# Second layers of a mixture of experts on one core: one product of 160 columns in place of two of 80, and a VectorE addition of the halves

## Chip, cores and metric

One Trainium2 chip, one core of it. The metric is the device time of one execution in microseconds (us). A profile is one such execution, recorded by the hardware; its times count from the start of the span.

## What is computed

Causal attention over 8 batches, 12 heads, 448 positions and 64 dimensions, in f32, and behind it a mixture of 8 experts over the 3584 resulting rows of 768:

```python
logits = x @ w_gate                       # 3584 x 8
expert_idx = np.argmax(logits, axis=1)    # one expert a row, softmax weight gate_w
for e in range(8):
    tok_idx = rows of expert e, at most the 80 with the largest gate_w
    h = np.maximum(x[tok_idx] @ w1[e], 0.0)             # 768 -> 1024, first layer
    out[tok_idx] = gate_w[tok_idx, None] * (h @ w2[e])  # 1024 -> 768, second layer
```

All other rows of the output are zero. The weights are f32, 768 x 1024 and 1024 x 768 an expert.

## The kernel before

**Two stages.** Up to about 325 us the core computes attention, the routing and the choice of rows; then it runs the experts' layers. The change lies in this second stage alone. There each layer is computed with weights as the stationary operand: TensorE loads a 128 x 128 block of a weight chunk (128 rows of the weight matrix, 1024 columns in a first layer, 768 in a second) and multiplies it with the 80 chosen tokens as 80 columns. A first layer has 6 chunks of 8 blocks, a second layer 8 chunks of 6 blocks.

**Split weights.** So as to multiply in f16 at f32 accuracy, weights and activations are split into a high and a low half. For a chunk ScalarE makes `wh` = f16(32 w) (L1203, "high"), VectorE makes `wl` = 32 w - wh (L1209, "low"). Of the tokens, `xh`/`xl` (first layer, L1443 and L1449) and `hh`/`hl` (second layer, L1460 and L1466) are the halves. Each block then takes three products of 80 columns, L1504 to L1506: `wh` with the high half, `wh` with the low half, `wl` with the high half, summed in PSUM. Each product is two TensorE instructions, a weight load and a matmul. The last chunk of seven layers (`WHOLE`) isn't split and goes as one f32 product a block (L1501).

**Around a layer.** Tokens are gathered by POOL (L1417) and turned by TensorE (`xtp`). A second layer's sum lies in one bank of PSUM, tile `op` (128 x 480, two buffers); ScalarE copies it to SBUF (`yt`, L1528), TensorE turns it back (`ytp`), ScalarE weights it (`yo`), POOL scatters it. The last expert (`last_layer`) does its last three chunks by halves of the output, and VectorE copies the second half (L1523).

**Buffers.** Raw weights come in pieces of three first-layer or four second-layer chunks into 11 buffers (L348, 74 loads in this stage, issued by SP); a load into a region waits until the high and low of the chunk that was there are made. There are 12 buffers for `wh` and 11 for `wl`; each is free when its chunk's products are done.

**Order.** `plan_experts` writes out the order of TensorE's, ScalarE's, VectorE's and SP's instructions by a simulation with the costs of the table `COST` (ns) and a due place in TensorE's order for each operation. TensorE's order of layers is first layer of expert 0, first of 1, second of 0, first of 2, second of 1 and so on: the layers of two experts alternate. On the chip each engine then runs its instructions in this order and waits on semaphores; so an operation that stands too early in an engine's order holds up all behind it.

Of the kernel before, what the change touches and what calls it, by code (L numbers as in the profile page):

```python
# [7 lines left out]
F32 = mybir.dt.float32  # L8
F32R = mybir.dt.float32r
F16 = mybir.dt.float16  # L10
BF16 = mybir.dt.bfloat16
I32 = mybir.dt.int32
AF = mybir.ActivationFunctionType
ALU = mybir.AluOpType
# [3 lines left out]
P = 128  # L18
# [30 lines left out]
ROW_ENGINES = "ppappppa"  # L49

COST = {"hi1": 950, "hi2": 735, "lo1": 1135, "lo2": 870, "xw": 210, "xh": 460, "xl": 575, "hw": 120, "hh": 330, "hl": 400,
        "yt": 470, "yo": 490, "xtp": 420, "ytp": 660, "warm": 600, "split": 108, "whole": 224, "ld": 460, "far": 2100, "seen": 100, "slack": 900}
BEGIN = {"ACT": 400, "SP": 1500, "DVE": 5900, "PE": 9400}
GATHERED, GATHERS = [9400, 12500, 14500], 6000

# [1 line left out]
def plan_experts(E, layers, blocks, order, whole, early, pieces, loaded, buffers, his, los, ready_h, ready_l):  # L57

    pe = [("xtp", 0), ("warm", 0)]
    for e, w in layers:  # L60
        for x, c in enumerate(order[e, w]):
            n = len(order[e, w])
# [7 lines left out]
    at = {op: i for i, op in enumerate(pe)}  # L70
    splits = [op[1:] for op in pe if op[0] == "p" and not whole(*op[1:]) and op[1:] not in early]
    ops, by = {}, []

    def add(op, engine, cost, needs, when):
        ops[op] = engine, COST[cost] if isinstance(cost, str) else cost, [d for d in needs if d], when
    used = {}
    for op in pe:
        if op[0] == "p":
            _, e, w, c = op
            o = whole(e, w, c)  # L80
            needs = [(("xw" if w == 1 else "hw") if o else ("xl" if w == 1 else "hl"), e), ("ld" if o else "lo", e, w, c)]
            if order[e, w][0] == c and e >= 2:
                needs.append(("hl" if w == 1 else "yt", e - 2))
            add(op, "PE", blocks[w] * COST["whole" if o else "split"], needs, at[op])
        elif op[0] == "warm":
            add(op, "PE", "warm", [], at[op])
        else:
            add(op, "PE", op[0], [("got", op[1]) if op[0] == "xtp" else ("yt", op[1])] + by, at[op])
            by = [("xl", op[1])] if op[0] == "xtp" else [("yo", op[1])]
    for e in range(E):  # L90
        for w, hi, lo, raw in ((1, "xh", "xl", "xw"), (2, "hh", "hl", "hw")):
            after = ("xtp", e) if w == 1 else ("p", e, 1, order[e, 1][-1])
            cs = {o: [at["p", e, w, c] for c in order[e, w] if whole(e, w, c) == o] for o in (False, True)}
            if cs[True]:
                add((raw, e), "ACT", raw, [after], min(cs[True]) - 0.5)
            if cs[False]:
                n = 2 if w == 2 else 1
                add((hi, e), "ACT", n * COST[hi], [after], min(cs[False]) - 0.7)
                add((lo, e), "DVE", n * COST[lo], [(hi, e)], min(cs[False]) - 0.5)
        if e < E - 1:  # L100
            add(("yt", e), "ACT", "yt", [("p", e, 2, order[e, 2][-1])], at["ytp", e] - 0.5)
            add(("yo", e), "ACT", 2 * COST["yo"], [("ytp", e)], at["ytp", e] + 4)
    done = {("lo", *y): 0 for y in early}
    for i, (e, w, c) in enumerate(splits):
# [17 lines left out]
    busy, times, ends, out, gathers = dict(BEGIN), set(BEGIN.values()), {}, [], len(GATHERED)  # L122
# [21 lines left out]
    while times:  # L144
        t = min(times)
# [4 lines left out]
        while empty and coming < len(pieces):  # L150
            held[coming] = empty.pop(0)
            e, w, cs = pieces[coming]
            for j, c in enumerate(cs):
                op = ("ld", e, w, c)
# [22 lines left out]
def attention_then_moe(  # L177
# [12 lines left out]
    nc = tc.nc  # L190
    B, _, NP, S = qT.shape
    N, D = out.shape
    E = wg.shape[2]
# [4 lines left out]
    NC1 = D // P  # L198
# [49 lines left out]
    SL = max(2, min(P, CAP))  # L248
# [9 lines left out]
    OFF, at = {}, 0  # L258
# [48 lines left out]
    def whole(e, which, c):  # L307

        return c == (NC1, NC2)[which - 1] - 1 and ((e, which) in WHOLE if AHEAD else e < E - which % 2 - 1)
# [3 lines left out]
    ORDER, sooner, PIECES = {}, [], []  # L313
    for x, (e, which) in enumerate(LAYERS):
        cs = sorted(range((NC1, NC2)[which - 1]), key=lambda c: (not whole(e, which, c), c))
        k = (K1, K2)[which - 1]
        if x in AHEAD:
            sooner.append((e, which, cs[:k]))
            PIECES.append((e, which, cs[k:]))
            cs = [c for both in zip(cs[:k], cs[k:]) for c in both]  # L320
        else:
            PIECES += [(e, which, cs[i:i + k]) for i in range(0, len(cs), k)]
        ORDER[e, which] = cs
    SOONER = [(e, which, c) for e, which, cs in sooner for c in cs]
    PIECES = sooner + PIECES
# [825 lines left out]
    n = len(pairs)  # L1151
# [33 lines left out]
    SW, SX = 32.0, 8.0  # L1185
# [5 lines left out]
    def source(y):  # L1191
        if y not in raw_of:
            i, j = place_of[y]
            raw_of[y] = chunk_of(wload[i], len(PIECES[i][2]), j)
        return raw_of[y]
# [48 lines left out]
    for i, pr in enumerate(pairs):  # L1244
# [13 lines left out]
        h = i // PH  # L1258
# [13 lines left out]
        _, first, afters = scores  # L1272
# [98 lines left out]
    for i, x in enumerate(ROW_ENGINES):  # L1371
        g, t = divmod(i, NT)
# [29 lines left out]
    ffn = ctx.enter_context(tc.tile_pool(name="ffn", bufs=2, side="right", reuse_waits="tile"))  # L1402
    ps_m = ctx.enter_context(tc.tile_pool(name="ps_m", bufs=2, space=PSUM, reuse_waits="tile"))
    ps = ctx.enter_context(tc.tile_pool(name="ps", bufs=2, space=PSUM, reuse_waits="tile"))
    NF = F // P
# [3 lines left out]
    PER = NC1 if NC1 * SL <= 512 else NC1 // 2  # L1409
# [12 lines left out]
    class Unit:  # L1422
# [32 lines left out]
            nc.scalar.activation(self.w2, self.hp[-1][:, HALF - n:], AF.Relu, scale=SW)  # L1455

        def hh(self):
            self.h2 = ffn.tile([P, NF, SL], F16, name="hh", tag="hh")
            for i, t in enumerate(self.hp):
                nc.scalar.activation(self.h2[:, i * HALF:(i + 1) * HALF], t, AF.Relu)  # L1460

        def hl(self):
            self.l2 = ffn.tile([P, NF, SL], F16, name="hl", tag="hl")
            for i, t in enumerate(self.hp):
                part = slice(i * HALF, (i + 1) * HALF)
                nc.vector.scalar_tensor_tensor(out=self.l2[:, part], in0=t, scalar=0.0, in1=self.h2[:, part], op0=ALU.max,  # L1466
                                               op1=ALU.subtract)

        def banks(self, which):
            if which == 1:  # L1470
                self.per = HALF
                self.hp = [ps.tile([P, HALF, SL], F32, name="hp", tag="h", bufs=4) for _ in range(2)]
                return self.hp
            final = self.e == E - 1
            self.per = NC1 // 2 if final else PER
            if final:
                self.op = [ps.tile([P, PER, SL], F32, name="op", tag="o")[:, 0:self.per],
                           ps.tile([P, HALF, SL], F32, name="hp", tag="h", bufs=4)[:, 0:self.per]]
            else:
                self.op = [ps.tile([P, self.per, SL], F32, name="op", tag="o", padded_shape=[P, PER, SL])  # L1480
                           for _ in range(NC1 // self.per)]
            return self.op

        def product(self, which, c, part=None):

            n = (NC1, NC2)[which - 1]
            blocks = (NF, NC1)[which - 1]
            x = ORDER[self.e, which].index(c)
            if x == 0 and not part:
                self.out = self.banks(which)  # L1490
            y = self.e, which, c
            if not whole(*y):
                h, l = (self.h1, self.l1) if which == 1 else (self.h2, self.l2)
                wh, wl = hi_of[y], lo_of[y]
            for i in part or range(blocks):
                o = self.out[i // self.per][:, i % self.per, :]
                ws = slice(i * P, (i + 1) * P)
                begin, end = x == 0 and i % self.per == 0, x == n - 1
                if whole(*y):
                    w = self.w1 if which == 1 else self.w2  # L1500
                    nc.tensor.matmul(o, source(y)[:, ws], w[:, w.shape[1] + c - n, :], start=begin, stop=end,  # L1501
                                     skip_group_check=True)
                    continue
                nc.tensor.matmul(o, wh[:, ws], h[:, c, :], start=begin, stop=False, skip_group_check=True)  # L1504
                nc.tensor.matmul(o, wh[:, ws], l[:, c, :], start=False, stop=False, skip_group_check=True)  # L1505
                nc.tensor.matmul(o, wl[:, ws], h[:, c, :], start=False, stop=end, skip_group_check=True)  # L1506

        def last_layer(self, c):
# [15 lines left out]

        def yt(self):
            self.y = ffn.tile([P, NC1, SL], F32, name="yt", tag="yt")
            for i, t in enumerate(self.op):
                nc.scalar.activation(self.y[:, i * self.per:(i + 1) * self.per], t, AF.Copy, scale=1.0 / (SW * SW * SX))  # L1528

        def ytp(self):  # L1530
            self.tp = []
# [22 lines left out]
    for s in range(NSL):  # L1554
# [7 lines left out]
        bufs = wload[0:BUFS]  # L1562
# [6 lines left out]
        for (kind, e, *y), info in turns:  # L1569
# [5 lines left out]
            elif kind == "ld":  # L1575
                b, i, j = info
# [7 lines left out]
            elif kind == "warm":  # L1584
                if PER == NC1:
                    warm = ps_m.tile([P, PER * SL], F32, name="wp", tag="misc")
# [53 lines left out]
```

## Time and profile before

| | us |
|---|---|
| median of 3 runs | 446.72 (446.46 to 448.32) |
| profiled execution | 446.64 |
| its span | 444.6 |
| TensorE busy in the span | 419.5 (94%) |
| ScalarE busy | 388.3 (87%) |
| VectorE busy | 379.3 (85%) |

The profiled execution is the one whose rows are shown; 2.04 us of it lie outside the span. Its granted TensorE clock is 0.994 of full speed, so the clock plays no part in what follows. The shares are means over two unlike stages; the stage of the experts is read by itself.

### The profile page before, as it was taken

Reading aid. Unit: us, or ns where it says so; the run is one execution under the profiler, and the core shown is the slowest. Engines: PE = TensorE matmul, PEld = TensorE weight load, DVE = VectorE, ACT = ScalarE, POOL = GpSimd, SP = SyncE. Lnnn points to the kernel's source line nnn. Section 1 sums busy time; section 2 is a strip of 40 time slices with the busy share of each in tenths; the row PEclk is TensorE's granted clock in tenths of the full one; section 3 lists DMA queues with packets and bytes.
Section 4 is the critical chain, followed back from the end, with each engine's and each line's share of the span. In section 5 each row is a group of like instructions: output and inputs, shape, how many; then the busy total and the mean of one; then the engine's idle time right before and its main releaser. Section 6 shows DMA issues by size and latency. Waiting matters only on the chain.

```text
span 444.6 us, 15877 instructions
## 1 busy us (share of the span) xinstructions
PE 419.5 (94%) x5847; PEld 325.2 (73%) x5847; DVE 379.3 (85%) x1302; ACT 388.3 (87%) x1062; POOL 286.9 (65%) x439
## 2 busy tenths in 40 slices
PE   7899999999999999999999999999789999888894
PEld 3666777677777777767777777766469999887893
DVE  6777788979889898988998989888879999989791
ACT  5899999999989999998999998978868979878891
POOL 7967998998898898899889885412462242210021
PEclk9899999999999999999999999999999999999999
DMA  7485668859786974976664387199359999999701
GB/s 224 147 272 184 195 227 285 291 201 295 241 282 199 290 242 152 297 253 212 214 215 144 124 243 272 66 349 312 126 171 349 403 403 411 393 414 413 306 27 46
DMA packets 49869, 109.95 MB, mean 247 GB/s; under 512 B 5970, under 2 KB 27474, under 8 KB 49152
## 3 DMA queue, kind: packets, MB, share of 16 engines
q1 hardware_dynamic: 48592, 105.20, 68.4%
q0 software_dynamic: 1056, 3.51, 2.4%
q8 instruction: 46, 0.75, 0.7%
q14 instruction: 31, 0.25, 0.2%
q10 hardware_dynamic: 144, 0.23, 0.2%
HBM read 85.35 MB, written 23.99 MB: 246 GB/s over the span
## 4 chain that ended last, share of the span: by engine, by line
PE 83%; ACT 5%; DVE 4%; issue 3%; POOL 2%; DMA 1%; POOLq 0%; DVEq 0%; ACTq 0%
PE xp L662 18%; PE tp L638 17%; PE sp L580 12%; PE rt L773 4%; ACT prob L603 4%; PE hp L1505 3%; PE hp L1506 3%; PE hp L1504 3%; PE op L1504 3%; PE op L1506 3%; PE op L1505 3%; PE gp L723 3%; PE sp L587 2%; PE hp L1501 2%; PE wp L1370 1%
## 5 line engine op out<-in xcount | busy, mean ns | idle before, releaser
L603 ACT ACTIVATE prob<-ns,nb 128x192 f32<-128x192 f32 (+3 forms) x336 | 175.5, 532 | 14.6 <-DVE nb L599 13.1
L599 DVE CUSTOM_DVE_ANT_0 ns<-sp,mask 128x192 f32<-128x192 f32 (+3 forms) x336 | 134.5, 443 | 17.7 <-PE sp L580 16.5
L638 PE MATMUL tp<-ident,prob 128*128 128x128 f32 x768 | 105.9, 279 | 0.1
L528 POOL TENSOR_TENSOR qk<-qk,qk 128x448 f16<-128x448 f32 x94 | 98.1, 1059 | 4.5 <-DVE qk L556 2.3
L1209 DVE SCALAR_TENSOR_TENSOR wl<-wraw,wh 128x768 f16<-128x768 f32 (+1 forms) x93 | 94.7, 1073 | 5.5 <-POOL wl L1566 2.1
L662 PE MATMUL xp<-PT,vt 128*64 128x448 f32 (+3 forms) x768 | 93.6, 386 | 0.2
L1203 ACT ACTIVATE wh<-wraw 128x768 f16<-128x768 f32 (+1 forms) x93 | 82.1, 941 | 12.3 <-PE hp L1505 5.9
L638 PEld LDWEIGHTS tp<-ident,prob 128*128 128x128 f32 x768 | 85.2, 142 | 3.2 <-ACT PT L643 0.5
L643 ACT COPY PT<-tp 128x512 f32<-128x512 f32 x144 | 77.0, 589 | 8.3 <-PE tp L638 7.0
L662 PEld LDWEIGHTS xp<-PT,vt 128*64 128x64 f32 x768 | 50.9, 136 | 44.7 <-issue 23.3
L580 PE MATMUL sp<-qk 64*128 64x448 f16 (+2 forms) x864 | 68.4, 297 | 2.9 <-POOL qk L528 1.8
L1506 PEld LDWEIGHTS <-wl 128*128 128x128 f16 x644 | 64.3, 100 | 3.9 <-issue 3.9
L603 ACT ACTIVATION_READ_ACCUMULATOR prob<-ns,nb 128x1 f32 x336 | 66.3, 197 | 0.0
L1504 PEld LDWEIGHTS <-wh 128*128 128x128 f16 x644 | 64.6, 100 | 1.7 <-issue 1.6
L1505 PEld LDWEIGHTS <-wh 128*128 128x128 f16 x644 | 64.3, 100 | 0.9 <-issue 0.8
L1550 POOL DMA_INDIRECT out<-yo,idx x8 | 15.6, 1954 | 69.4 <-ACT yo L1547 65.0
L580 PEld LDWEIGHTS <-qk 64*128 64x128 f16 x864 | 36.5, 94 | 17.7 <-issue 2.9
L643 DVE COPY PT<-tp 64x256 f32<-64x256 f32 x144 | 43.6, 328 | 2.9 <-PE tp L638 0.8
L1505 PE MATMUL hp<-xl,wh 128*128 128x80 f16 x344 | 38.8, 202 | 2.1 <-DVE xl L1449 1.2
L1506 PE MATMUL hp<-xh,wl 128*128 128x80 f16 x344 | 38.8, 202 | 1.1 <-issue 1.1
L1504 PE MATMUL hp<-xh,wh 128*128 128x80 f16 x344 | 38.9, 202 | 0.0
L556 POOL CAST qk<-qk 128x896 f16<-128x896 f32 x40 | 36.2, 935 | 0.4
(198 smaller groups left out, 734.7 us busy)
## 6 DMA issues: line engine op xcount, KB each, us to landing
wraw<-w SPq DMA_DIRECT2D x45, 384.0 KB
wraw<-w SPq DMA_DIRECT2D x31, 512.0 KB
out<-mask SPq DMA_DIRECT2D x56, 192.0 KB
qk<-k_t SPq DMA_DIRECT2D x23, 448.0 KB
qk<-q_t SPq DMA_DIRECT2D x23, 448.0 KB
vt<-v_t SPq DMA_DIRECT2D x24, 384.0 KB
xs<-xr SPq DMA_DIRECT2D x42, 192.0 KB
wraw<-w SPq DMA_DIRECT2D x24, 192.0 KB
```

What stands on the lines that cost most here:

```text
L528: sub = lambda e, o, a, b: e.tensor_tensor(out=o, in0=a, in1=b, op=ALU.subtract)
L580: nc.tensor.matmul(pr.sp[t, j], a[rows, p, queries(t)], c[rows, p, FROM[t]:FROM[t] + WIDTH[t]], start=(x == 0), stop=(x == 2))
L599: nc.vector.tensor_tensor_reduce(out=ns, in0=pr.sp[x], in1=m, scale=-1.0 / 8.0, scalar=HUGE, op0=ALU.add, op1=ALU.min, accum_out=nb)
L603: nc.scalar.activation(pr.P[:, OFF[x]:OFF[x] + w], got[0], AF.Exp, bias=got[1], scale=-1.0, accum_out=pr.sums[:, h:h + 1])
L638: nc.tensor.transpose(tp[:, i * P:(i + 1) * P], f, ident)
L643: way(part_of(pr.PT, rows, to, *todims), part_of(got[0], rows, at, *dims))
L662: nc.tensor.matmul(xp[rows, to:to + w], st["vt"][:, c, p * P + j * DH:p * P + (j + 1) * DH], pr.PT[:, j, n0:n0 + w], start=(c == 0), stop= ...
L1203: nc.scalar.activation(hi_of[y][:, 0:src.shape[1]], src, AF.Copy, scale=SW)
L1209: nc.vector.scalar_tensor_tensor(out=lo_of[y][:, 0:n], in0=src, scalar=SW, in1=hi_of[y][:, 0:n], op0=ALU.mult, op1=ALU.subtract)
L1504: nc.tensor.matmul(o, wh[:, ws], h[:, c, :], start=begin, stop=False, skip_group_check=True)
L1505: nc.tensor.matmul(o, wh[:, ws], l[:, c, :], start=False, stop=False, skip_group_check=True)
L1506: nc.tensor.matmul(o, wl[:, ws], h[:, c, :], start=False, stop=end, skip_group_check=True)
```

## The change

Seven of the eight experts (not the last) compute the split chunks of the second layer with two products a block in place of three: `hh` and `hl` now lie in one tile (`both`), and one matmul multiplies `wh` with both halves as 2 x 80 = 160 columns, into two places of a PSUM bank; the second multiplies `wl` with the high half as before, into the first place. The `op` tile so takes two banks and has one buffer where there were two: the next second layer can begin only when the sum of the one before was read in full, not of the one before that. `yt` copies the first places on ScalarE, and a new VectorE instruction `ya` (128 x 480, one operand in PSUM, one in SBUF) adds the second ones. The planner gets a cost for `ya` and puts it right behind the `yt` of its expert.

Apart from that, the very first piece of split weights now takes its chunks in rising order, [0, 1, 2], where it had [5, 0, 1]. The pieces that come after reuse its buffer, so a load that goes there follows other chunks' splitting.

```diff
--- before.py
+++ after.py
@@ -49,7 +49,7 @@
 ROW_ENGINES = "ppappppa"
 
 COST = {"hi1": 950, "hi2": 735, "lo1": 1135, "lo2": 870, "xw": 210, "xh": 460, "xl": 575, "hw": 120, "hh": 330, "hl": 400,
-        "yt": 470, "yo": 490, "xtp": 420, "ytp": 660, "warm": 600, "split": 108, "whole": 224, "ld": 460, "far": 2100, "seen": 100, "slack": 900}
+        "yt": 470, "ya": 600, "yo": 490, "xtp": 420, "ytp": 660, "warm": 600, "split": 108, "whole": 224, "ld": 460, "far": 2100, "seen": 100, "slack": 900}
 BEGIN = {"ACT": 400, "SP": 1500, "DVE": 5900, "PE": 9400}
 GATHERED, GATHERS = [9400, 12500, 14500], 6000
 
@@ -79,13 +79,13 @@
             _, e, w, c = op
             o = whole(e, w, c)
             needs = [(("xw" if w == 1 else "hw") if o else ("xl" if w == 1 else "hl"), e), ("ld" if o else "lo", e, w, c)]
-            if order[e, w][0] == c and e >= 2:
-                needs.append(("hl" if w == 1 else "yt", e - 2))
+            if order[e, w][0] == c and e >= 3 - w:
+                needs.append(("hl", e - 2) if w == 1 else ("ya", e - 1))
             add(op, "PE", blocks[w] * COST["whole" if o else "split"], needs, at[op])
         elif op[0] == "warm":
             add(op, "PE", "warm", [], at[op])
         else:
-            add(op, "PE", op[0], [("got", op[1]) if op[0] == "xtp" else ("yt", op[1])] + by, at[op])
+            add(op, "PE", op[0], [("got", op[1]) if op[0] == "xtp" else ("ya", op[1])] + by, at[op])
             by = [("xl", op[1])] if op[0] == "xtp" else [("yo", op[1])]
     for e in range(E):
         for w, hi, lo, raw in ((1, "xh", "xl", "xw"), (2, "hh", "hl", "hw")):
@@ -99,6 +99,7 @@
                 add((lo, e), "DVE", n * COST[lo], [(hi, e)], min(cs[False]) - 0.5)
         if e < E - 1:
             add(("yt", e), "ACT", "yt", [("p", e, 2, order[e, 2][-1])], at["ytp", e] - 0.5)
+            add(("ya", e), "DVE", "ya", [("yt", e)], at["ytp", e] - 0.4)
             add(("yo", e), "ACT", 2 * COST["yo"], [("ytp", e)], at["ytp", e] + 4)
     done = {("lo", *y): 0 for y in early}
     for i, (e, w, c) in enumerate(splits):
@@ -319,7 +320,8 @@
             PIECES.append((e, which, cs[k:]))
             cs = [c for both in zip(cs[:k], cs[k:]) for c in both]
         else:
-            PIECES += [(e, which, cs[i:i + k]) for i in range(0, len(cs), k)]
+            at = cs if PIECES else sorted(cs)
+            PIECES += [(e, which, at[i:i + k]) for i in range(0, len(cs), k)]
         ORDER[e, which] = cs
     SOONER = [(e, which, c) for e, which, cs in sooner for c in cs]
     PIECES = sooner + PIECES
@@ -1455,12 +1457,12 @@
             nc.scalar.activation(self.w2, self.hp[-1][:, HALF - n:], AF.Relu, scale=SW)
 
         def hh(self):
-            self.h2 = ffn.tile([P, NF, SL], F16, name="hh", tag="hh")
+            self.both = ffn.tile([P, 2, NF, SL], F16, name="hh", tag="hh")
+            self.h2, self.l2 = self.both[:, 0], self.both[:, 1]
             for i, t in enumerate(self.hp):
                 nc.scalar.activation(self.h2[:, i * HALF:(i + 1) * HALF], t, AF.Relu)
 
         def hl(self):
-            self.l2 = ffn.tile([P, NF, SL], F16, name="hl", tag="hl")
             for i, t in enumerate(self.hp):
                 part = slice(i * HALF, (i + 1) * HALF)
                 nc.vector.scalar_tensor_tensor(out=self.l2[:, part], in0=t, scalar=0.0, in1=self.h2[:, part], op0=ALU.max,
@@ -1471,15 +1473,14 @@
                 self.per = HALF
                 self.hp = [ps.tile([P, HALF, SL], F32, name="hp", tag="h", bufs=4) for _ in range(2)]
                 return self.hp
-            final = self.e == E - 1
-            self.per = NC1 // 2 if final else PER
-            if final:
-                self.op = [ps.tile([P, PER, SL], F32, name="op", tag="o")[:, 0:self.per],
+            self.per = NC1 // 2
+            t = ps.tile([P, 2, 512], F32, name="op", tag="o", bufs=1)
+            if self.e == E - 1:
+                self.op = [t[:, 0, 0:self.per * SL].rearrange("k (c s) -> k c s", s=SL),
                            ps.tile([P, HALF, SL], F32, name="hp", tag="h", bufs=4)[:, 0:self.per]]
-            else:
-                self.op = [ps.tile([P, self.per, SL], F32, name="op", tag="o", padded_shape=[P, PER, SL])
-                           for _ in range(NC1 // self.per)]
-            return self.op
+                return self.op
+            self.op = t[:, :, 0:NC1 * SL].rearrange("k g (x n) -> k g x n", x=2)
+            return [t[:, g, 0:NC1 * SL].rearrange("k (x c s) -> k c x s", x=2, s=SL) for g in range(2)]
 
         def product(self, which, c, part=None):
 
@@ -1491,18 +1492,24 @@
             y = self.e, which, c
             if not whole(*y):
                 h, l = (self.h1, self.l1) if which == 1 else (self.h2, self.l2)
+                joined = which == 2 and self.e < E - 1
                 wh, wl = hi_of[y], lo_of[y]
             for i in part or range(blocks):
-                o = self.out[i // self.per][:, i % self.per, :]
+                o = self.out[i // self.per][:, i % self.per]
                 ws = slice(i * P, (i + 1) * P)
                 begin, end = x == 0 and i % self.per == 0, x == n - 1
+                if which == 2 and self.e < E - 1:
+                    two, o = o, o[:, 0]
                 if whole(*y):
                     w = self.w1 if which == 1 else self.w2
                     nc.tensor.matmul(o, source(y)[:, ws], w[:, w.shape[1] + c - n, :], start=begin, stop=end,
                                      skip_group_check=True)
                     continue
-                nc.tensor.matmul(o, wh[:, ws], h[:, c, :], start=begin, stop=False, skip_group_check=True)
-                nc.tensor.matmul(o, wh[:, ws], l[:, c, :], start=False, stop=False, skip_group_check=True)
+                if joined:
+                    nc.tensor.matmul(two, wh[:, ws], self.both[:, :, c, :], start=begin, stop=False, skip_group_check=True)
+                else:
+                    nc.tensor.matmul(o, wh[:, ws], h[:, c, :], start=begin, stop=False, skip_group_check=True)
+                    nc.tensor.matmul(o, wh[:, ws], l[:, c, :], start=False, stop=False, skip_group_check=True)
                 nc.tensor.matmul(o, wl[:, ws], h[:, c, :], start=False, stop=end, skip_group_check=True)
 
         def last_layer(self, c):
@@ -1524,8 +1531,13 @@
 
         def yt(self):
             self.y = ffn.tile([P, NC1, SL], F32, name="yt", tag="yt")
-            for i, t in enumerate(self.op):
-                nc.scalar.activation(self.y[:, i * self.per:(i + 1) * self.per], t, AF.Copy, scale=1.0 / (SW * SW * SX))
+            y = self.y.rearrange("k (g c) s -> k g (c s)", g=2)
+            nc.scalar.activation(y, self.op[:, :, 0], AF.Copy, scale=1.0 / (SW * SW * SX))
+
+        def ya(self):
+            y = self.y.rearrange("k (g c) s -> k g (c s)", g=2)
+            nc.vector.scalar_tensor_tensor(out=y, in0=self.op[:, :, 1], scalar=1.0 / (SW * SW * SX), in1=y, op0=ALU.mult,
+                                           op1=ALU.add)
 
         def ytp(self):
             self.tp = []
```

TensorE's order where expert 0's second layer begins (`op` is its sum, `hw`, `hh` and `hl` its tokens whole, high and low), before:

```order
L1501 MATMUL op<-hw,wraw 128x80 x6
L1504 LDWEIGHTS wh_6695
L1504 MATMUL op<-hh,wh_6695 128x80
L1505 LDWEIGHTS wh_6695
L1505 MATMUL op<-hl,wh_6695 128x80
L1506 LDWEIGHTS wl_6707
L1506 MATMUL op<-hh,wl_6707 128x80
```

and of the kernel changed:

```order
L1505 MATMUL op<-hw,wraw 128x80 x6
L1509 LDWEIGHTS wh_6695
L1509 MATMUL op<-hh,wh_6695 128x2x80
L1513 LDWEIGHTS wl_6707
L1513 MATMUL op<-hh,wl_6707 128x80
```

A block takes four instructions in place of six; over the seven experts it is 324 blocks, 648 instructions fewer, and nothing is added on TensorE.

VectorE's order at the end of the stage (`hl`, in the changed kernel written into a part of `hh`, is the last expert's low half of the tokens; `wl` of 128 x 768 are its second layer's chunks), before:

```order
L1466 SCALAR_TENSOR_TENSOR hl<-hp,hh 128x320 x2
L1209 SCALAR_TENSOR_TENSOR wl_6705<-wraw,wh_6404 128x768
L1209 SCALAR_TENSOR_TENSOR wl_6706<-wraw,wh_6405 128x768
L1209 SCALAR_TENSOR_TENSOR wl_6707<-wraw,wh_6697 128x768
L1209 SCALAR_TENSOR_TENSOR wl_6406<-wraw,wh_6698 128x768
L1209 SCALAR_TENSOR_TENSOR wl_6407<-wraw,wh_6699 128x768
L1209 SCALAR_TENSOR_TENSOR wl_6408<-wraw,wh_6691 128x768
L1209 SCALAR_TENSOR_TENSOR wl_6700<-wraw,wh_6692 128x768
L1209 SCALAR_TENSOR_TENSOR wl_6701<-wraw,wh_6693 128x768
L1523 TENSOR_SCALAR yt<-hp 128x240
```

and changed:

```order
L1468 SCALAR_TENSOR_TENSOR hh<-hp,hh 128x320 x2
L1211 SCALAR_TENSOR_TENSOR wl_6705<-wraw,wh_6404 128x768
L1211 SCALAR_TENSOR_TENSOR wl_6706<-wraw,wh_6405 128x768
L1539 SCALAR_TENSOR_TENSOR yt<-op,yt 128x480
L1211 SCALAR_TENSOR_TENSOR wl_6707<-wraw,wh_6697 128x768
L1211 SCALAR_TENSOR_TENSOR wl_6406<-wraw,wh_6698 128x768
L1211 SCALAR_TENSOR_TENSOR wl_6407<-wraw,wh_6699 128x768
L1211 SCALAR_TENSOR_TENSOR wl_6408<-wraw,wh_6691 128x768
L1211 SCALAR_TENSOR_TENSOR wl_6700<-wraw,wh_6692 128x768
L1211 SCALAR_TENSOR_TENSOR wl_6701<-wraw,wh_6693 128x768
L1530 TENSOR_SCALAR yt<-hp 128x240
```

The `ya` of expert 6 now stands between the second and the third of the last eight lows, and six lows are queued behind it. In the same way the `ya` of expert 5 stands ahead of the last low of 128 x 1024:

```order
L1211 SCALAR_TENSOR_TENSOR wl_6704<-wraw,wh_6404 128x1024
L1211 SCALAR_TENSOR_TENSOR wl_6705<-wraw,wh_6405 128x1024
L1211 SCALAR_TENSOR_TENSOR wl_6706<-wraw,wh_6697 128x1024
L1539 SCALAR_TENSOR_TENSOR yt<-op,yt 128x480
L1211 SCALAR_TENSOR_TENSOR wl_6707<-wraw,wh_6698 128x1024
L1468 SCALAR_TENSOR_TENSOR hh<-hp,hh 128x320 x2
```

Behind this `ya` the whole second layer of expert 6 and of the last expert is still to be split. On ScalarE the `yt` of expert 6, which had one `wh` behind it, now stands behind the last `wh`.

## Rows read from the trace of the kernel before

**Rows 1.** The page's head.

```profile
span 444.6 us, 15877 instructions
```

**Rows 2.** Chain that ended last, 343 to 437.5 us: start, us, what.

```profile
by line: PE op L1504 13.8%; PE op L1506 13.7%; PE op L1505 13.2%; PE hp L1506 11.3%; PE hp L1505 11.3%; PE hp L1504 11.0%; issue 9.0%; PE hp L1501 5.8%; PE ytp L1537 5.0%; PE op L1501 2.9%; PE xtp L1433 2.8%; DVE yt L1523 0.4%
...
348.35 0.38 issue
...
384.34 1.28 issue
...
420.31 1.08 issue
...
437.37 0.42 DVE yt L1523
```

**Rows 3.** Windows: us, PE PEld DVE ACT POOL busy (instructions), PEclk, DMA share, GB/s.

```profile
385.61:391.60 5.99, 4.98 (x128) 4.84 (x128) 4.79 (x7) 3.18 (x5) 0.73 (x1) 1.00 1.02 415
...
397.52:403.50 5.98, 4.96 (x128) 4.86 (x129) 5.45 (x7) 5.70 (x9) 0.84 (x1) 1.00 1.02 415
425.00:435.00 10.00, 10.00 (x272) 9.99 (x269) 9.61 (x13) 8.57 (x14) 3.17 (x2) 1.00 0.10 28
```

**Rows 4.** The page's DMA queues: packets, MB, share of 16 engines.

```profile
q8 instruction: 46, 0.75, 0.7%
```

**Rows 5.** DMA queues in 389.2 to 390.4 us.

```profile
q8 instruction: 1, 0.02, 5.0%
```

**Rows 6.** Windows of the experts' stage.

```profile
325.80:434.61 108.81, 99.13 (x2287) 96.28 (x2285) 102.21 (x115) 91.30 (x136) 26.85 (x14) 1.00 0.87 334
343.00:421.40 78.40, 69.97 (x1650) 68.59 (x1646) 71.80 (x80) 67.37 (x100) 15.53 (x8) 1.00 1.00 397
...
434.61:437.16 2.55, 2.55 (x76) 2.55 (x74) 0.00 (x1) 0.37 (x1) 0.79 (x1) 1.00 0.35 97
```

**Rows 7.** What VectorE waited for, 325.8 to 437 us: total, times, longest.

```profile
DVE xl L1449 <- ACT xh L1443: 3.2, 2, 2.0
...
DVE wl L1209 <- issue: 0.8, 2, 0.6
DVE wl L1209 <- ACT wh L1203: 0.8, 1, 0.8
DVE wl L1209 <- ACT yo L1547: 0.6, 2, 0.3
DVE wl L1209 <- PE hp L1506: 0.5, 1, 0.5
```

**Rows 8.** VectorE's timeline: start, us, what.

```profile
402.63 0.65 DVE L1449 SCALAR_TENSOR_TENSOR xl<-xtp,xh 128x480 f16<-128x480 f32 x1
403.20 1.21 DVE L1209 SCALAR_TENSOR_TENSOR wl<-wraw,wh 128x1024 f16<-128x1024 f32 x1
...
417.91 1.22 DVE L1209 SCALAR_TENSOR_TENSOR wl<-wraw,wh 128x1024 f16<-128x1024 f32 x1
...
427.58 7.03 DVE L1209 SCALAR_TENSOR_TENSOR wl<-wraw,wh 128x768 f16<-128x768 f32 x8
```

**Rows 9.** ScalarE's timeline.

```profile
420.03 0.58 ACT L1528 ACTIVATE yt<-op 128x480 f32<-128x480 f32 x1
...
432.01 0.84 ACT L1203 ACTIVATE wh<-wraw 128x768 f16<-128x768 f32 x1
```

**Rows 10.** What SP's queue waited for, 320 to 420 us.

```profile
SPq L348 <- DVE wl L1209: 10.5, 13, 5.1
```

**Rows 11.** SP's timeline from 322 us on.

```profile
327.05 87.30 SPq L348 DMA_DIRECT2D wraw<-w  x74
```

**Rows 12.** Windows: the start of the stage and the end of the loads.

```profile
324.00:326.00 2.00, 2.00 (x12) 1.07 (x11) 0.20 (x1) 2.00 (x3) 1.25 (x3) 1.00 0.00 0
...
420.00:425.00 5.00, 3.92 (x97) 3.78 (x94) 5.00 (x6) 5.00 (x9) 0.20 (x1) 1.00 0.09 31
```

**Rows 13.** POOL's timeline, 322 to 330 us.

```profile
325.65 0.12 POOL L1566 MEMSET wl<- 128x1 f16 x1
```

## The prediction, made blind

> **What bounds the kernel now.** I read the engines' shares first, saw that they mix two unlike stages, and took the experts' stage by itself. The profiled execution took 446.64 us, of which the span is 444.6 [rows 1]; what lies outside, 2.04 us, I leave as it is.
>
> Second came the chain of waits from 343 to the end of the products. It lies on TensorE nearly whole: product lines, a few turns, and nothing of VectorE, ScalarE or DMA but the last `yt` [rows 2]. So TensorE ends last here, though VectorE is the busier beside it: 71.80 against 69.97 us of 78.40 [rows 6]. What to see is the word "issue" with 9.0% of that stretch, about 8.5 us: time in which TensorE waited for no semaphore. It comes in ten pieces, of which three are shown [rows 2], 0.10 to 1.28 us each, about every 6 us.
>
> Third, I cut the time at three neighbouring pieces. Between two of them lie 128 matmuls and 128 weight loads, 256 instructions, in 5.99 and 5.98 us, at a DMA share of 1.02 [rows 3]. Without weight traffic the same engine does 272 products in 10.00 us, 0.0368 us each with all turns among them [rows 3], so 128 need 4.7 us. A stretch of 256 instructions thus takes 1.2 to 1.3 us more than its work while the DMA engines are full, and nothing more when they are idle. There is a DMA queue of instructions, 46 packets with 0.75 MB in the execution, 16.3 KB each [rows 4]; one of its packets runs right ahead of a stall [rows 5]. I take it that TensorE waits for its own next 256 instructions, which come through full DMA engines. With DMA full TensorE so gets 256 instructions in about 6 us whatever they do, and the number of its instructions is a price of its own.
>
> Last, I read VectorE's waits. From 325.80, the first low of the stage, to 434.61, the last one's end, are 108.81 us, with 102.21 busy [rows 6]: 6.6 us idle. Of these 3.2 are `xl` behind `xh`, which waits for TensorE's turn; 0.8 follow a high, 0.6 a `yo`, 0.5 a product; 0.8 are issue [rows 7]. So VectorE stands little behind TensorE in length, and most of its idle time comes from TensorE being late.
>
> **The change part by part.**
>
> *TensorE.* 324 blocks lose one weight load and one matmul: 648 instructions, 2.5 stretches of 256. An expert has 6 x 8 blocks in each layer; less the unsplit ones it goes from about 600 to 504 instructions, 14.0 to 11.8 us at 6 us for 256. A product of 160 columns isn't in the trace. It can't be under one of 80 (0.037) nor, I reason, over two (0.074), as the columns are as many. I take the upper end, nearest to columns; then 64 blocks of a second layer, a full stretch of 256 instructions, carry 64 x 0.110 = 7.1 us of work, more than the 6 us of the instructions' arrival, and no stall is left in them. At the lower end the stall stays but the work falls further. Either way TensorE gains some 2 us an expert against before, if nothing else holds it, over six experts more than VectorE can follow. So TensorE stops being the bound, and its gain isn't the gain of the kernel.
>
> *VectorE.* Seven `ya` of 128 x 480, one operand in PSUM and one in SBUF. The nearest row is `xl`, the same size and the same kind of operands: 0.65 us, and the next instruction begins 0.57 after its start [rows 8]. 7 x 0.57 = 4.0 us. The bounds: 0.5 each if the f32 output costs less, the 0.65 of the row in full if nothing overlaps, 3.5 to 4.6. They lie on what is now the path. `yt` on ScalarE stays one instruction of 480 columns; I cost it at nothing, since it only reads the columns from two banks.
>
> *What VectorE regains.* With TensorE ahead, the waits that come from it go: 3.2 + 0.8 + 0.6 + 0.5 = 5.1 us, in six waits. At a restart the overlap of 0.08 us (0.65 - 0.57) is lost too, so 6 x 0.08 = 0.5 more. Not regained I count the 0.8 of issue and the rest. Last low: 434.61 + 4.0 - 5.6 = 433.0, or 1.6 earlier. The bounds: nothing regained (+4.0), all 6.6 with its restarts regained (about 7.8, so -3.8).
>
> *The end.* At 434.61 TensorE still has 76 products to do, in 2.55 us, 0.0336 each [rows 6]. What must follow the last low are the last expert's last chunk in the first half of the output (9 products) and three chunks of the second (27): 36 x 0.0336 = 1.2 us. If TensorE is no longer behind, 1.3 us go. Then come the last `yt` and the write, as before.
>
> *The bank with one buffer.* The next second layer's first product waits for `ya` of the expert before. A whole first layer lies between, 48 blocks or over 5 us, against 0.6 + 0.6 for `yt` and `ya`: nothing, unless VectorE is more than 4 us late with `ya`.
>
> *`ya` in VectorE's order.* It waits for `yt`, hence for the end of a second layer, and all lows behind it wait along: one low of 128 x 1024, then the last layers' lows for expert 5, six lows for expert 6. With TensorE ahead `yt` is done before; I count nothing. The price without that cover is the first rival.
>
> *First piece in rising order.* SP's longest wait for a low is 5.1 us, until the first load of the stage goes at 327.05 [rows 10, 11]. In rising order two loads of 384 KB can go about 5 us earlier, while the DMA engines are idle (share 0.00 from 324 to 326 [rows 12]). Worth: nothing. The loads end by about 422 (share 0.09 from 420 to 425 [rows 12]), and the last high starts at 432.01 [rows 9], ten us later. Against it: they run beside the first gather, and the first low follows POOL's memset at 325.65 [rows 13]. 786 KB at 0.4 MB/us are 1.9 us, the most that could be lost.
>
> **Sum.** +4.0 (`ya`) - 5.6 (VectorE's idle time) - 1.3 (end) = -2.9 us; 446.64 - 2.9 = 443.7. The profiled execution lies 0.08 under the median, 446.72, so this stands for the median too.
>
> **Rivals.**
>
> *A late `ya` holds up the lows (slower).* If TensorE isn't relieved, `yt` of expert 5 ends at 420.03 + 0.58 = 420.61 [rows 9] and `ya` at 421.18. Behind it stands the last low of 128 x 1024, which before began at 417.91 [rows 8]: 3.27 later. With the `ya` of expert 6 all behind it lies 3.8 later, the last low ends at 438.4, and 1.2 us of products follow: 439.6 against 437.16, +2.5, 449.1 us. It decides where `yt` of expert 5 comes later than about 417.3. For it: VectorE's longest waits even now follow TensorE. Against it: the stalls in [rows 2, 3], which must shrink with fewer instructions.
>
> [...]
>
> *Half relieved (same).* TensorE gains, but stalls of 1.2 us stay (the packets come even later, say), or VectorE finds other waits; it regains about the 4.0 it spends. Then only the end gives something: 445.4 to 446.7.
>
> *The early loads cost (same).* They delay gather and first low by up to the 1.9 us: 443.7 + 1.9 = 445.6. For it: the gather is small and stands on the path of the whole stage. Against: SP's issue of one load isn't POOL's.
>
> **Chances.** The forecast 0.62; half relieved 0.19; early loads 0.08; late `ya` 0.11. What a measurement of this kernel can tell from no change is about 0.5%, 2.2 us: faster is under 444.5, slower over 448.9. So faster 0.62, same 0.27, slower 0.11. The range: at the low end all of VectorE's idle time regained at the cheaper `ya` (3.5 - 7.8 - 1.3 = -5.6, 441.0); at the high end half relieved with nothing regained at the end, 447.0. For the forecast alone, 441.0 to 444.5.
>
> **What would show it.** The "issue" pieces gone from the chain in the second layers, and the chain from 343 on VectorE rather than TensorE; VectorE's busy share from 325.8 to its last low 0.97 or more; `xl` no longer waiting for `xh`; `ya` near 0.6 us each, with no wait ahead of it; 36 to 40 products behind the last low; SP's first load near 322. Wrong: stalls of over 1 us still every 256 instructions of a second layer, or waits of over 1 us of `ya` for `yt`.

## The result, and the profile after

The changed kernel takes 442.22 us (median; 441.15 to 442.98) against 446.85 us, a ratio of 0.9889 with a 95% interval of 0.9858 to 0.9919: 4.6 us faster by the medians. Forecast were 443.7, in a range of 441.0 to 447.0. The profiled execution took 441.15 us, 5.5 less than that of before. One execution of the kernel with five experts joined, below, took 1105 us; it was the profiled one, and it is left out with its trace.

The page's head after (first the span, then busy us, share and instructions) answers to [rows 1]; the last line is that of before:

```profile
span 439.4 us, 15220 instructions
...
PE 419.4 (95%) x5523; PEld 324.0 (74%) x5523; DVE 382.7 (87%) x1309; ACT 386.9 (88%) x1062; POOL 312.3 (71%) x439
...
q8 instruction: 43, 0.70, 0.6%
```

```profile
PE 419.5 (94%) x5847; PEld 325.2 (73%) x5847; DVE 379.3 (85%) x1302; ACT 388.3 (87%) x1062; POOL 286.9 (65%) x439
```

TensorE has 324 weight loads and 324 matmuls fewer, VectorE 7 instructions more, and the queue of instructions moved three packets fewer than in [rows 4]. TensorE's busy time over the whole span stayed the same; its instructions' number is what fell.

The windows of the stage after, with the columns of [rows 3]: from VectorE's first low to the end of its last, the stretch in which TensorE stalled before, and the end. They answer to [rows 6]:

```profile
325.69:430.61 104.92, 101.01 (x2007) 97.38 (x2005) 104.91 (x122) 90.07 (x136) 51.39 (x14) 1.00 0.89 339
343.00:421.40 78.40, 77.31 (x1563) 76.12 (x1561) 78.40 (x92) 75.32 (x114) 39.36 (x9) 1.00 0.98 387
430.61:432.09 1.48, 1.43 (x36) 1.44 (x37) 0.00 (x1) 0.37 (x1) 0.78 (x1) 1.00 0.17 50
```

VectorE works 104.91 of 104.92 us. Its 6.6 us of idle time are gone, all of them. Behind its last low lie just the 36 products of the forecast. TensorE isn't far ahead: it works 77.31 of the 78.40 us, and its step from one product to the next is 35 to 37 ns for 80 columns and 70 for 160 there, so these are work and not small waits. Of the whole stretch it is idle for 3.9 us (104.92 less 101.01), 2.4 of them in one wait near the end, shown further below.

What TensorE's weight loads waited for from 343 to 421.4 us (total, times, longest), where the chain of before had its ten pieces of "issue" [rows 2]; before:

```profile
PEld L1506 <- issue: 3.6, 4, 1.2
PEld L1505 <- issue: 3.1, 3, 1.4
PEld L1504 <- issue: 1.6, 2, 1.1
PEld ytp L1537 <- issue: 1.3, 1, 1.3
```

and after:

```profile
PEld ytp L1549 <- DVE yt L1539: 1.1, 2, 0.8
PEld L1513 <- DVE wl L1211: 0.6, 3, 0.2
PEld L1513 <- issue: 0.2, 1, 0.2
```

Of 9.6 us 0.2 are left, and what is waited for now is VectorE. Two blocks of a second layer in the chain, start, us, what:

```profile
344.44 0.07 PE op L1509
344.51 0.04 PE op L1513
344.54 0.07 PE op L1509
344.61 0.04 PE op L1513
```

A block takes 0.10 to 0.11 us, nearly what three products of 0.0368 did: the 160 columns cost almost what two of 80 did (0.070 us). So 64 blocks, 256 instructions, carry some 6.7 us of work (64 x 0.105), longer than the 6 us in which instructions came before.

`ya` in VectorE's timeline (start, us, what):

```profile
349.83 0.94 DVE L1211 SCALAR_TENSOR_TENSOR wl<-wraw,wh 128x768 f16<-128x768 f32 x1
350.69 0.65 DVE L1539 SCALAR_TENSOR_TENSOR yt<-op,yt 128x480 f32<-128x480 f32 x1
351.26 1.81 DVE L1211 SCALAR_TENSOR_TENSOR wl<-wraw,wh 128x768 f16<-128x768 f32 x2
```

0.65 us, 0.57 to the next start, and nothing waited ahead of it: `xl` [rows 8] was the right row to price it by.

The chain that ended last, from 343 us on, is a lesson in how not to read it:

```profile
by line: DMA wraw<-w 26.2%; DVE wl L1211 20.8%; PE op L1509 10.2%; PE hp L1505 6.1%; PE op L1513 5.7%; issue 5.0%; PE hp L1512 4.9%; PE hp L1513 4.7%; PE hp L1511 4.7%; PE op L1505 3.1%; PE ytp L1549 2.2%; DVE hh L1468 2.1%; PE xtp L1435 1.
```

It names the weight loads first. But VectorE had no idle time, so no load can have held it; with TensorE, VectorE and ScalarE busy for 77.31, 78.40 and 75.32 of the 78.40 us above, the chain wandered among them and the loads. With a quarter of the loads' bytes the changed kernel's time stayed as it was (second experiment).

### The profile page after: what moved, and what is told of

It is laid out like the page before. It is cut to its first block, busy times and chain, and to the rows that moved or that the text cites. A ratio compares the mean times of both kernels' runs of the same rounds, so it can differ in the third digit from the quotient of the medians.

```text
span 439.4 us, 15220 instructions
## 1 busy us (share of the span) xinstructions
PE 419.4 (95%) x5523; PEld 324.0 (74%) x5523; DVE 382.7 (87%) x1309; ACT 386.9 (88%) x1062; POOL 312.3 (71%) x439
## 4 chain that ended last, share of the span: by engine, by line
PE 78%; DVE 9%; DMA 6%; ACT 2%; POOL 2%; issue 2%; POOLq 0%; DVEq 0%; SPq 0%; ACTq 0%
PE xp L664 20%; PE tp L640 19%; PE sp L582 14%; DMA wraw<-w 5%; DVE wl L1211 4%; PE rt L775 4%; PE gp L725 3%; PE op L1509 2%; PE hp L1505 2%; PE sp L589 2%; PE hp L1512 2%; PE hp L1513 2%; PE hp L1511 2%; PE wp L1372 2%; ACT prob L605 1%
## 5 line engine op out<-in xcount | busy, mean ns | idle before, releaser
L640 PEld LDWEIGHTS tp<-ident,prob 128*128 128x128 f32 x768 | 84.2, 141 | 3.2 <-ACT PT L645 0.5
L1562 POOL DMA_INDIRECT out<-yo,idx x8 | 40.1, 5010 | 43.0 <-ACT yo L1559 39.9
L1512 PEld LDWEIGHTS <-wh 128*128 128x128 f16 x392 | 39.1, 100 | 2.5 <-issue 2.5
L1511 PEld LDWEIGHTS <-wh 128*128 128x128 f16 x392 | 39.3, 100 | 0.0
```

The costliest lines, as they stand in the source:

```text
L640: nc.tensor.transpose(tp[:, i * P:(i + 1) * P], f, ident)
```

## The experiments

**Three products again, all else as changed.**

```diff
-nc.tensor.matmul(two, wh[:, ws], self.both[:, :, c, :], start=begin, ...)
+nc.tensor.matmul(two[:, 0], wh[:, ws], h[:, c, :], start=begin, ...)
+nc.tensor.matmul(two[:, 1], wh[:, ws], l[:, c, :], start=False, ...)
```

> The changed kernel, but with three products of 80 columns a block again (wh with the high half, wh with the low half, wl with the high half); halves in two places, ya, the bank with one buffer and the first piece stay. Theory (the number of TensorE's instructions is the price while DMA is full): the 648 instructions are back, TensorE stalls at every 256 again in the second layers, it becomes the bound, and ya now waits for a late yt: 447 to 450 us, VectorE idle 5 us or more between its first and last low of the stage. Rival (the gain comes from the product's work: one of 160 columns is shorter than two of 80): by the traces a block takes 0.104 us with 160 columns and 0.108 with three products, 324 x 0.004 = 1.3 us, so at most 443.5 us.

Measured: 450.92 us, 1.0074 (1.0052 to 1.0096) of the kernel before (447.31 on that chip), 0.9 over the expected range. TensorE's stalls are back; the stretch from the end of one to the end of the next has 256 instructions, with the columns of [rows 3]:

```profile
386.17:392.14 5.97, 4.95 (x128) 4.85 (x128) 4.45 (x7) 3.19 (x5) 2.28 (x1) 1.00 1.03 418
```

From the first low to the last one's end, and what VectorE waited for there:

```profile
326.48:439.71 113.23, 103.31 (x2301) 98.92 (x2300) 105.53 (x122) 91.07 (x136) 23.05 (x14) 0.98 0.83 315
```

```profile
DVE xl L1451 <- ACT xh L1445: 4.3, 2, 2.7
DVE yt L1540 <- ACT yt L1536: 3.4, 3, 1.7
DVE wl L1211 <- POOL wl L1579: 1.9, 1, 1.9
```

VectorE is idle for 7.7 us (113.23 less 105.53), the first two lines; the third wait ends with the first low, ahead of the stretch. `ya` waits for `yt` three times: this is the first rival of the forecast, alive as soon as TensorE isn't relieved. The kernel is 3.6 us slower than before, where the rival's price was +2.5. The same columns in 648 more instructions cost 8.3 us of the stage (113.23 against 104.92), as by the ratios (1.0074 - 0.9889, or 8.3 us). The rival of work, which allowed 443.5 us at most, falls.

**A quarter of the weight traffic, in the kernel before and in the changed one.** Each load of the stage brings only the first quarter of its chunk's columns; the rest of the chunk is what lay in the buffer.

```diff
+m = w // less   # less = 4 in the loads of the experts' stage
-nc.sync.dma_start(chunk_of(t, len(cs), j)[:, x * w:(x + 1) * w], ...)
+nc.sync.dma_start(chunk_of(t, len(cs), j)[:, x * w:x * w + m], ...)
```

> The kernel before, but each load of the experts' stage brings only the first quarter of its chunk's columns (so the stage works in part on the numbers of earlier chunks; all other work stays). Theory (TensorE's instructions wait behind full DMA engines): the issue stalls of about 1.2 us at every 256 instructions go with the weight traffic, VectorE is the bound without any ya, last low near 427 us and the whole 437 to 439 us. Rival (a crossing of 256 instructions costs that whatever DMA does, or DMA wasn't the cause): 446 to 447 us.

> The changed kernel with the same loads of a quarter. Theory: VectorE has no idle time left to lose in the changed kernel, so nothing changes: 441.5 to 442.5 us, slower than the kernel before with quarter loads by about the seven ya, 4.0 us. Rival (the changed kernel still loses time to stalls or to loads): 439 us or less.

Measured, against 447.31 us for the kernel before on that chip: before with a quarter 438.40 us, 0.9796 (0.9777 to 0.9816); changed with a quarter 442.61, 0.9894 (0.9852 to 0.9936), 0.1 over the expected range. From the first low to the last one's end, before with a quarter:

```profile
326.55:427.75 101.20, 100.67 (x2331) 98.08 (x2329) 101.05 (x115) 89.65 (x136) 45.57 (x14) 1.00 0.41 115
```

and changed with a quarter:

```profile
326.74:431.66 104.92, 100.09 (x1974) 97.07 (x1973) 104.91 (x122) 90.08 (x136) 50.20 (x14) 0.98 0.38 108
```

With a DMA share of 0.41 the kernel before has no stall: TensorE's longest wait from 343 us on is 0.5 us, for a low. Both engines are full now, VectorE with 101.05 and TensorE with 100.67 of the 101.20 us. The changed kernel doesn't gain at all, 104.92 us as with full loads. With a quarter of the traffic the change is a loss of 4.2 us (3.7 in these two stretches), about the seven `ya`. So its whole gain comes from stalls that the kernel before had at a DMA share of 1.00 [rows 6] and not, in the same 343 to 421.4 us, at 0.39. That these are instructions arriving slowly, and not products or weight loads slowed by the traffic, is inferred from where they lie: in the trace of before the ten stalls lie 254 to 256 recorded products and weight loads apart, or a multiple of it (some records are missing; in the earlier ones of the stage, not every such distance shows a stall). Whether such a packet waits in the DMA engines' queues or in memory no run here tells.

**Fewer experts joined.** The rule "all but the last" becomes "from k on, but the last"; the others have three products into one place and no `ya`.

```diff
-joined = which == 2 and self.e < E - 1
+joined = which == 2 and FIRST_JOINED <= self.e < E - 1   # 1, 2, 4
```

> The changed kernel, but expert 0 has its three products of 80 into one place again, and no ya: six experts joined. Theory (VectorE, never idle, is the bound of the changed kernel; TensorE has some us in hand): one ya less, -0.6 us against the changed kernel, 441.6 us. Rival (TensorE has nothing in hand): its 96 instructions at 6 us for 256 are 2.2 us, 444 us.

> The same for experts 0 and 1: five joined. Theory: two ya less, -1.1 us, 441.1 us, if TensorE's 4.5 us more are still in hand, else up to 443 us. Rival (nothing in hand): 446 us.

> The same for experts 0 to 3: three joined. Theory: TensorE has 9 us more to do, more than it has in hand; it is late for the lows and for the ya that are left: 443 to 446 us, VectorE idle 3 us or more. Rival (the number of TensorE's instructions isn't the price; VectorE alone sets the end): four ya less, 440 us.

> The changed kernel once more, beside the three others on one chip: 442.2 us, within 0.5.

Measured, as ratios to the kernel before on that chip (446.17 us): seven joined 0.9911 (0.9891 to 0.9931), 441.62 us; six 0.9903 (0.9886 to 0.9920), 441.47; five 0.9925 (0.9903 to 0.9946), 442.13; three 1.0002 (0.9984 to 1.0019), 446.23. Seven, the changed kernel again, came 0.6 us under the 442.2 expected, a little outside the 0.5 allowed. From first to last low, six joined:

```profile
325.22:429.67 104.45, 100.39 (x2048) 97.43 (x2045) 104.43 (x121) 89.94 (x136) 46.82 (x14) 1.00 0.89 341
```

and three, with what VectorE waited for then (325 to 432 us):

```profile
326.76:434.03 107.27, 99.85 (x2156) 96.75 (x2154) 103.60 (x118) 90.36 (x136) 31.40 (x14) 1.00 0.87 332
```

```profile
DVE wl L1219 <- issue: 2.5, 2, 1.9
DVE xl L1459 <- ACT xh L1453: 1.5, 2, 1.2
DVE wl L1219 <- ACT yo L1574: 0.6, 2, 0.3
DVE wl L1219 <- PE hp L1525: 0.5, 1, 0.5
DVE wl L1219 <- ACT wh L1213: 0.2, 1, 0.2
```

One `ya` less shortens the stage by 0.47 us while TensorE has time in hand; in the whole time this can't be told from noise. With four less VectorE's busy time falls by 1.3 us only (104.91 to 103.60), as overlaps are lost at restarts, it is idle for 3.7, and the gain is gone: 446.23 us, a little over the 443 to 446 of the theory and far from the rival's 440. Of the first line's 2.5 us, 1.9 are the wait that ends with the first low, ahead of the stretch; 0.6 lie in it.

What TensorE's weight loads waited for with three joined, from 343 to 399 us:

```profile
PEld L1525 <- issue: 2.1, 2, 1.1
PEld L1523 <- issue: 1.4, 1, 1.4
PEld L1524 <- issue: 1.0, 2, 0.8
```

and from 399 us, about where the first joined product runs (399.1), to 427 us:

```profile
PEld L1524 <- issue: 0.3, 1, 0.3
```

So within one execution the stalls lie where the second layers have three products, 4.5 us against 0.3, though the DMA share from 399 to 421 us is still 0.92.

Five came out 1.0 us over the 441.1 of the theory, within the 443 that it allowed if TensorE hasn't 4.5 us in hand. The changed kernel's 3.9 us of idle TensorE speak for that, but the intervals of five, six and seven overlap, so it isn't shown. None of these beats the changed kernel by what can be measured.

**POOL adds the halves.** ScalarE copies both to SBUF in one instruction, POOL adds them, VectorE has no `ya`.

```diff
-nc.scalar.activation(y, self.op[:, :, 0], AF.Copy, scale=...)
-nc.vector.scalar_tensor_tensor(out=y, in0=self.op[:, :, 1], ..., in1=y, ...)
+nc.scalar.activation(t, self.op.rearrange("k g x n -> k g (x n)"), AF.Copy, scale=...)
+nc.gpsimd.tensor_tensor(out=t[:, :, 0:h], in0=t[:, :, 0:h], in1=t[:, :, h:], op=ALU.add)
```

> The changed kernel with the addition of the halves on POOL: ScalarE copies both halves (128 x 960) in one yt, POOL adds them in SBUF, VectorE has no ya. Theory (VectorE is the bound throughout): its 7 x 0.57 us go, 438.2 us plus what ScalarE's longer copies cost (7 x 0.4 us beside its idle time: nothing). Rival (ScalarE, TensorE or the loads are as near to the bound as VectorE, or POOL's addition slows VectorE's lows): 441 us or more.

Measured: 467.47 us, 1.0405 (1.0332 to 1.0478) of the kernel before. POOL's additions in its timeline:

```profile
351.94 8.19 POOL L1535 TENSOR_TENSOR yt<-yt 128x480 f32<-128x480 f32 x1 [1.41 <-ACT yt L1533]
...
373.20 1.95 POOL L1535 TENSOR_TENSOR yt<-yt 128x480 f32<-128x480 f32 x1 [3.07 <-ACT yt L1533]
...
405.03 1.20 POOL L1535 TENSOR_TENSOR yt<-yt 128x480 f32<-128x480 f32 x1 [8.70 <-ACT yt L1533]
```

and VectorE's beside the first two:

```profile
350.99 8.09 DVE L1210 SCALAR_TENSOR_TENSOR wl<-wraw,wh 128x768 f16<-128x768 f32 x8
363.38 1.23 DVE L1210 SCALAR_TENSOR_TENSOR wl<-wraw,wh 128x1024 f16<-128x1024 f32 x1 [4.31 <-issue]
...
374.00 1.96 DVE L1210 SCALAR_TENSOR_TENSOR wl<-wraw,wh 128x768 f16<-128x768 f32 x1
```

The same addition takes 1.20 us or 8.19. The long one ends at 360.13, one us after VectorE's series of eight lows ended at 359.08; so do three others of the seven, each 1.05 to 1.06 us after a series. The one at 373.20 got in between two lows, and there a low took 1.96 us in place of 0.95. So in this run the two engines held each other up; by what means no run tells. In the meantime TensorE waits for the addition (`ytp` for POOL's `yt`, 20.7 us in seven waits), and VectorE in the end for all. Behind such a wait the granted clock fell as well, to 0.50 from 360.2 to 364 us after TensorE had stood for most of 8 us, so a part of the loss may be the clock's; how large a part, no run tells.

The theory that VectorE is the bound isn't touched by this; that POOL could take its work in this form is refuted.

**The first piece alone, and the change without it.**

```diff
-PIECES += [(e, which, cs[i:i + k]) for i in range(0, len(cs), k)]
+at = cs if PIECES else sorted(cs)
+PIECES += [(e, which, at[i:i + k]) for i in range(0, len(cs), k)]
```

> The kernel before with the first piece of split chunks in rising order, and nothing else. Theory: SP's first load goes at about 322 us, loads land earlier, and the time doesn't move, as they landed about ten us before use: 446.8 us, within 0.5. Rival (the loads' start is a part of the gain): 445 us or less; rival (they delay the first gather): 448 us or more.

> The changed kernel with the first piece in the old order [5, 0, 1]. Theory: as the changed kernel, 442.2 us within 0.5. Rival (the earlier loads help once TensorE and VectorE are faster): 443 us or more.

Measured, against 446.81 us for the kernel before on that chip: alone 445.97 us, 0.9976 (0.9958 to 0.9993), 0.3 below the expected range; the change without it 442.66, 0.9896 (0.9866 to 0.9925). In the changed kernel it gives nothing that shows. Alone it may give up to 1.9 us by the interval; the middle, 1.1, is below the 0.5% that I can tell. In its profile the stretch from first to last low took 108.99 us, 0.18 more than before, so none of it lies there. The loads do start earlier; SP's timeline of the changed kernel, against [rows 11]:

```profile
321.85 0.91 SPq L350 DMA_DIRECT2D wraw<-w  x2
```

VectorE's first low began at 325.69, against 325.80 before. Over eleven profiles it began at 324.6 to 326.9 us with the early loads and, in three without, at 325.8 to 328.0: they didn't hold it up.

## Why the prediction was right, and where its sizes were off

**Who bounds.** Right. TensorE's stalls at every 256 instructions (from 378 us on at each, before that at some) were the bound, and they belong to the instructions' number under full DMA: shown by putting the instructions back (+8.3 us) and by taking the traffic away (-8.9 us in the kernel before, nothing in the changed one). From 343 to 421.4 us the weight loads of the kernel before show "issue" waits of 9.6 us in ten pieces, up to 1.4 us each, at a DMA share of 1.00 [rows 6]; with quarter loads, at 0.39, they show none.

**TensorE's gain.** Right that it is enough, too large in size. The 160 columns came near the upper end, two of 80, and the stalls went all the same. But the 2 us an expert counted 6 us for every 256 instructions, also where the prediction itself has 7.1 us of work in them; by the 6.7 measured a second layer goes at its work's pace. TensorE ended up idle for 3.9 us of the stage, about half a us an expert, as VectorE set the pace.

**`ya`.** 7 x 0.57 = 4.0 us, as said: the two kernels with quarter loads, in which VectorE has hardly any idle time, differ by 3.9 us of its busy time (104.91 less 101.05).

**What VectorE regains.** The mis-sized step. From first to last low the stage went from 108.81 [rows 6] to 104.92: -3.9 us, where -1.6 was forecast. With 4.0 for `ya`, 7.9 were regained, not 5.6: the whole 6.6 of idle time where 5.1 were counted, and 1.3 for overlaps lost at restarts where 0.5 were: VectorE stood still 14 times in that stretch, half of them for under 0.28 us, and not six times. The second is borne out by the kernel before with quarter loads: the same 115 instructions kept VectorE busy for 101.05 us without stalls and for 102.21 with them. I had kept 0.8 of "issue" and the small rest of [rows 7] as not TensorE's. They were gone as well, and with three experts joined one wait under the name "issue" was back (0.6 us). So the name of a wait that ends last doesn't say that its cause lies elsewhere. The forecast's lower bound for this step (7.8, -3.8) was what happened.

**The end.** 2.76 us from the last low to the last `yt` (434.61 [rows 6] to 437.37 [rows 2]) became 1.48, -1.3 as said. With -0.1 for the start of the stage the sum is -5.3; the span fell by 5.2, and the median by 4.6, where -2.9 was forecast.

**The bank with one buffer.** Right in price, wrong in its reason. Between the second layers of the last two experts there is no first layer. There TensorE waited for `ya` of expert 6:

```profile
PE op L1511 <- DVE yt L1539: 2.4, 1, 2.4
```

In this execution it cost nothing, because VectorE's lows set the end, and 36 products were left behind the last one. But in two of the five profiles with six or seven experts joined and `ya` on VectorE, that of the changed kernel with quarter loads and that without the early loads, the granted clock fell to 0.50 behind this same wait of 2.4 us. More products were then left, and the end took 2.36 and 2.47 us in place of 1.48. With quarter loads, in the columns of [rows 3]:

```profile
427.00:429.00 2.00, 2.00 (x32) 2.00 (x31) 2.00 (x4) 0.00 (x0) 0.00 (x0) 0.50 0.00 0
431.66:434.02 2.36, 2.36 (x67) 2.36 (x64) 0.00 (x1) 0.37 (x1) 0.78 (x1) 1.00 0.36 103
```

So the one buffer can cost 0.9 to 1.0 us at the end; why the clock held in the other three no run tells.

**The late `ya`.** It didn't come. The first experiment showed that its condition was TensorE's lateness.

**The chain on VectorE.** Not shown as I wrote it; the chain went through loads, and VectorE's busy share (1.00) had to tell.

## What to carry over

Here TensorE stood for up to 1.28 us [rows 2] at 256 instructions while weights streamed at a DMA share of about 1.0, and 648 instructions were worth 8.3 us. In a kernel like this one count the instructions of the engine that issues most of them: look for idle time named "issue" at equal counts of instructions, and try fewer and longer ones before fewer columns. Then price the new work on the engine that is next: what can come back is its idle time and the overlaps lost at its restarts (6.6 and 1.3 us here). When one bound is removed, let the forecast's range take in all of that, whatever the waits are named.

## What the runs showed of the hardware

POOL was the slower here, the less VectorE stood idle. From first to last low POOL's 14 instructions were busy for 23.05 us where VectorE was idle for 7.7, 26.85 at 6.6, 31.40 at 3.7, and 45.57 to 51.39 where it had next to no idle time (times on POOL are rough). The addition of 128 x 480 took 1.20 to 8.19 us, and the changed kernel's own scatters, which mean 1.95 us of POOL each before, became

```profile
L1562 POOL DMA_INDIRECT out<-yo,idx x8 | 40.1, 5010 | 43.0 <-ACT yo L1559 39.9 <-DVE yo L1561 3.1
```

5.01 us, without harm here since VectorE's lows set the end; with POOL's addition on the path the kernel became 4% slower.

Over eleven profiled executions, before among them, the first low began between 324.6 and 328.0 us, a spread of 3.4 us that doesn't follow the change; the stretch from first to last low repeated within 0.02 us (104.92, 104.92 with quarter loads and without the early loads, 104.94 in the repeat). For differences below one per cent that stretch was the sharper measure.
